# Group sums by identity products, reciprocals back in two transfers, and a planner that counts instruction blocks

## The chip, the core and the metric

The kernel runs on one core of a Trainium2 chip. The metric is the device time of one execution in microseconds, the median of the runs shown. Five engines take part: TensorE (PE; its weight loads are listed as PEld), VectorE (DVE), ScalarE (ACT), GpSimd (POOL) and SyncE (SP), which only issues transfers. Each runs its own list of instructions in order and waits on semaphores for the others.

## The reference

Two stages. The first is an attention with two parts per head (8 batches, 8 heads, 576 tokens, 64 columns); the second is an MLP over all 4608 tokens.

```
q_d, k_d, v_d = means over groups of 4 tokens             # 144 rows
out_d    = softmax(q_d k_d^T / 8) v_d, each row repeated 4 times
local    = softmax(q k^T / 8 where |i - j| < 4, else -1e9) v
x        = out_d + local            -> (4608, 512)
h        = x w_in                   # w_in (512, 2048)
out      = (h * sigmoid(h)) w_out   # w_out (2048, 512)
```

## The kernel before

The 64 heads are worked on in 32 pairs, two heads on the two halves of 128 rows. For a pair p the jobs have these names in the code:

- T: 36 transposes of q and k into PSUM (L807); e: the two copies of them to the tiles qT and kT (L837); for the first 12 pairs (GS_PE) also the sums over groups of 4 tokens, in the same PSUM banks, as 60 small matmuls against a permuted identity (idp, L809 to L824), copied to qd and kd (jobs mq, mk, L843). Later pairs form these sums on VectorE from qT and kT (L852).
- S: the scores (L866); x and xd: the exponentials on ACT (L897), tiles Pt and Pd.
- Z: the row sums of the exponentials by 14 matmuls (L955); r: their reciprocals on VectorE, tile zr (L969).
- PV: the products with v (L935, L948); m: the multiply of PV's result by the reciprocals, tile xo (L1020), which also frees PV's two PSUM banks; a: the sum of both parts on POOL into xT (L1047), the input of the MLP.

The multiply needs the reciprocals spread over rows and columns, tile Rb. The first 8 pairs (RB_PE) do that on TensorE: two corrections of zr on VectorE (L973), 20 matmuls (L994) and a copy (L1004). All later pairs do it by two transfers that ACT issues: zr to a scratch in DRAM (scr, L980), and, once that has landed, scr to Rb (L983). The source pattern of the second is 2 halves x 64 repeats x 720 numbers.

The MLP is cut into 9 blocks of 512 tokens. A G1 job is 4 matmuls of 128x512 (L1068), a tanh on ACT (th, L1073) and a product on VectorE (gT, L1077), which frees its PSUM bank; apart from the first and last block only two banks serve G1. A G2 job is 4 matmuls of 128x512 (L1098); 16 matmuls form one result, which ACT copies (osb, L1105) and SP stores.

Pairs 0 to 7 run as separate jobs. From pair 8 on, a visit V(n) on TensorE holds S of n, T of n+1, Z of n-1 and PV of n-2, and about 8 MLP jobs of 4 matmuls stand between two visits. PV and Z of a visit use one pair of banks (CD), so a visit can't begin its PV before the multiply of the previous visit's pair has run.

The order on every engine is written out when the kernel is built: a planner (class Plan, its loop at L324 to L476) takes jobs with costs, due times (D, L52) and pools of buffers, plays them through and appends each job's instructions to its engine's list. Nothing is reordered when it runs. Loads of q, k and v come from SP in the order of load_order (L99), with gates; three pairs of q and k and all weights come from POOL's queue. While TensorE is idle early on, the planner puts in matmuls on a constant tile (dz, L1273 to L1277).

All matmuls of TensorE but the transposes are recorded by one helper, so they have the line L557; copies have L551, transfers L671.

Of the kernel before, what the change touches and what calls it, by code (L numbers as in the profile page):

```python
# [20 lines left out]
WARM_END, WARM_GAP, WARM_PART = 115.0, 0.4, 0.6  # L21
# [12 lines left out]
K_ENG = "DVE"  # L34
FRESH = 2.2


def Z_ENG(p):
    return "ACT"
# [12 lines left out]
def D(p, left):  # L52
    return (22 + 2 * (p - 3) if p < 4 else 42 + 3 * (p - 7) if p < 8 else 45 + 8 * (p - 7)) - left
# [45 lines left out]
def load_order():  # L99
    o = ["kx", ("qk", 0), ("qk", 1), ("qk", 2), ("qk", 3), ("v", 0), ("v", 1), ("v", 2), ("v", 3)]  # L100
    for p in range(4, NPAIR):
        o += [("qk", p), ("v", p)] + ([("vq", p)] if p >= VP_PE else [])
    return o, {1: ["ck1"], **{p: ["lv311!"] for p in range(4, 8)}, 8: ["w2"]}
# [8 lines left out]
def LD_ENG(x, p):  # L112
    return "SP"
# [129 lines left out]
class Job:  # L243
    __slots__ = ("name", "eng", "cost", "emit", "pre", "take", "use", "due", "work", "port", "kind", "bank", "marks", "gran",
                 "idx", "n", "succ", "start", "end", "ran", "last", "thr", "idle")

    def __init__(self, name, eng, cost, emit, **kw):
# [7 lines left out]
        self.ran, self.last, self.succ, self.end, self.idle = None, None, [], None, None  # L255


class Plan:
# [65 lines left out]
    def run(self, pick):  # L324
# [25 lines left out]
        busy = {e: 0.0 for e in Prog.ENGS}  # L350
        ported = {"DVE": 0.0, "POOL": 0.0}
        queues = {e: [] for e in Prog.ENGS}
        fluid = [0.0, 0]
# [60 lines left out]
        def dispatch(e, now):  # L414
# [14 lines left out]
            if e == "PE":  # L429
                b = min((b for b in range(8) if self.banks[b] is None), key=lambda b: self.freed[b], default=None)  # L430
                if b is not None:
                    j.idle = (now - max(busy["PE"], self.freed[b]), b)
            self.grab(j)
            start = now
            if j.port and e in ported:
                start = max(now, ported["POOL" if e == "DVE" else "DVE"])
            j.ran, j.start = e, now
            cost = j.cost[e] * (COLD[1] if e == "PE" and now < COLD[0] else 1.0)
            end = start + cost
            busy[e] = end  # L440
# [21 lines left out]
        at(0.0, lambda: None)  # L462
# [16 lines left out]
def bass_hourglass_attn__then__act_silu_kernel(  # L479
# [9 lines left out]
    with kctx:  # L489
# [37 lines left out]
        zr = sb("zr", [128, 72], F32, N_ZR)  # L527
        Rb = sb("Rb", [128, 720], F32, N_RB)
# [16 lines left out]
        idp = sb("idp", [128, 64], BF16)  # L545
# [25 lines left out]
        kx, rkx = region(2048, 576)  # L571
        cpv = cp.rearrange("p (a b) -> p a b", a=2)
# [3 lines left out]
        def col(i):  # L576
            return cv[:, i:i + 1]
# [16 lines left out]
        def fill(name, parts, due, eng=("DVE", "POOL")):  # L594
            def emit(j):
                for dst, val, r, w in parts:
                    P.op(j.ran, lambda e, dst=dst, val=val: e.memset(dst, val), r, w)
            J(name, eng, {"DVE": 0.07 * len(parts), "POOL": 0.14 * len(parts)}, emit, due=due)

        def constants():  # L600
# [5 lines left out]
            ts("ch", col(CH), col(CP_), 64.0, ALU.is_ge, 1.0, ALU.mult, rc(CP_), rc(CH), 0.07, ["cp"], -100)  # L606
            ts("cb", col(CB), col(CH), -64.0, ALU.mult, 0.0, ALU.add, rc(CH), rc(CB), 0.07, ["ch"], -99)
            ts("cwb", col(CW), col(CH), 224.0, ALU.mult, -4.5, ALU.add, rc(CH), rc(CW), 0.07, ["ch"], -95)
            ts("ck", col(CK), col(CP_), col(CB), ALU.add, 0.0, ALU.add, rc(CP_, CB), rc(CK), 0.07, ["cb"], -95)
            ts("idn", idn[:, :], ci, col(CB), ALU.add, 0.0, ALU.is_equal, rc(CB) + ri, [R("idn")], 0.15,  # L610
               ["ci", "cb"], -98)
            ts("coa", col(CO), col(CK), 3.0, ALU.is_ge, 1.0, ALU.mult, rc(CK), rc(CO), 0.07, ["ck"], -50)
            ts("co2", col(CO2), col(CK), 58.5, ALU.is_le, col(CO), ALU.mult, rc(CK, CO), rc(CO2), 0.07, ["coa"], -50)
            ts("co", col(CO), col(CK), 60.5, ALU.is_le, col(CO), ALU.mult, rc(CK, CO), rc(CO), 0.07, ["co2"], -50)
            ts("ce0", col(CE0), col(CP_), 3.0, ALU.is_ge, 1.0, ALU.mult, rc(CP_), rc(CE0), 0.07, ["cp"], -60)
            ts("ce1", col(CE1), col(CP_), 123.0, ALU.is_lt, 1.0, ALU.mult, rc(CP_), rc(CE1), 0.07, ["cp"], -60)
            ts("ga", col(GA), col(CK), 10.0, ALU.is_ge, -1.0, ALU.mult, rc(CK), rc(GA), 0.07, ["ck"], -40)
            ts("gb", col(GB), col(CK), 20.0, ALU.is_ge, -1.0, ALU.mult, rc(CK), rc(GB), 0.07, ["ck"], -40)

            def size(name, x, b, rx, rb, cost, pre, due):  # L620
# [4 lines left out]
            const("gsel", "DVE", 0.12, lambda e: e.tensor_copy(idp[:, :].rearrange("p (b a) -> p b a", b=4),  # L625
                                                               idn[:, :].rearrange("p (a b) -> p b a", b=4)),
                  r=[R("idn")], w=[R("idp")], pre=["idn"], due=-90)
            for i, (a, b, c, rr) in enumerate(((0, 58, col(CE0), rc(CE0)), (58, 232, 1.0, []),
                                               (232, 288, col(CE1), rc(CE1)))):
                ts(f"mask{i}", mask[:, a:b], cm[:, a:b], 3.0, ALU.is_le, c, ALU.mult, rr + rm, [R(f"mask{i}")], 0.15,  # L630
                   ["cma"] + (["ce0", "ce1"] if rr else []), -20)
            ts("cm0", col(CM0), col(CK), 3.0, ALU.is_lt, 100.0, ALU.mult, rc(CK), rc(CM0), 0.07, ["ck"], -94)
            ts("cm1", col(CM1), col(CK), 59.0, ALU.is_ge, 100.0, ALU.mult, rc(CK), rc(CM1), 0.07, ["ck"], -94)
            ts("nidn", nidn[:, :], idn[:, :], -81920.0, ALU.mult, 0.0, ALU.add, [R("idn")], [R("nidn")], 0.1, ["idn"], -85)
            for i, (y, a, b, c) in enumerate(((0, 0, 58, CM0), (0, 58, 288, None), (1, 0, 232, None), (1, 232, 288, CM1))):
                if c is None:
                    ts(f"mb{i}", mbias[:, y, a:b], cm[:, a:b], 3.0, ALU.is_gt, 1.0, ALU.mult, rm, [R(f"mb{i}")], 0.25,
                       ["cma"], -84)
                else:
                    ts(f"mb{i}", mbias[:, y, a:b], cm[:, a:b], col(c), ALU.add, 3.0, ALU.is_gt, rc(c) + rm, [R(f"mb{i}")],  # L640
                       0.12, ["cma", "cm0", "cm1"], -84)
            for i, c in enumerate((CO, CO, CO2)):
                ts(f"vsel{i}", vsel[:, i, :], cpv[:, i % 2, :], 1.5, ALU.is_le, col(c), ALU.mult, rc(c) + rp,
                   [R(f"vsel{i}")], 0.22, ["cpa", "co", "co2"], -70)
            ts("rsela", rsel[:, :], idn[:, 0:10], 1.0, ALU.mult, 0.0, ALU.add, [R("idn")], [R("rsel")], 0.07, ["idn"], -60)
            for i in (1, 2):
                const(f"rsel{i}", "DVE", 0.07, lambda e, i=i: e.tensor_tensor(
                    rsel[:, :], rsel[:, :], idn[:, 10 * i:10 * i + 10], ALU.add), r=[R("idn"), R("rsel")],
                    w=[R("rsel")], pre=["rsela" if i == 1 else "rsel1"], due=-60)
# [5 lines left out]
                 + [(hot[64 * j:64 * j + 16, 2, 13 + 5 * j:34 + 5 * j:10], 4.0, [rW[2]], [rW[2]]) for j in range(2)], -72,  # L655
                 "DVE")
            fill("ohf", [(ohf[:, 0:30], 0.0, [], [R("ohf")]), (ohf[:, 30:64], 1.0, [], [R("ohf2")])]
                 + [(ohf[half(j), 5 * j:5 * j + 21:10], 1.0, [R("ohf")], [R("ohf")]) for j in range(2)], -71, "DVE")
# [139 lines left out]
        def pe_T(p):  # L798
            a, b = S("qkb", p), S("qkb", p - 1)
            grp = p < GS_PE  # L800
# [8 lines left out]
            if grp:  # L809
                for r in range(9):  # L810
                    cs = [(9 * b_ + r) // 4 for b_ in range(4)]
                    runs, b0 = [], 0
                    for b_ in range(1, 5):
                        if b_ == 4 or cs[b_] - cs[b_ - 1] != 2:
                            runs.append((b0, b_))
                            b0 = b_
                    for a_, e_ in runs:
                        for j, h, x, n in tiles:
                            t = t_home(p, x, 0)[0]
                            o = PS[half(h), t, 288:432].rearrange("p (c a) -> p c a", c=9)  # L820
                            c0 = cs[a_]
                            mm(o[:, c0:c0 + 2 * (e_ - a_) - 1:2, :], qkb[n][half(j), x, 64 * r:64 * r + 64],
                               idp[half(j), 16 * a_:16 * e_].rearrange("p (b a) -> p b a", a=16),
                               [R("idp"), R(f"qkb{n}{x}")], [rB[t]], r == 0, r == 8)  # L824

        def after_T(p):
# [12 lines left out]
            def group(x):  # L839
                def emit(jb):  # L840
                    s, b = S("T", p), bank(("qk"[x], p))[0]
                    dst = qd[s][:, :] if x == 0 else kd[s][:, 0:SD]
                    P.op(jb.ran, lambda e: copy(jb.ran, e, dst.rearrange("p (a c) -> p a c", c=9),  # L843
                                                PS[:, b, 288:432].rearrange("p (c a) -> p a c", c=9)),
                         [rB[b]], [R(f"{'qk'[x]}d{s}")])
# [9 lines left out]

            for x in range(2):
# [3 lines left out]
                if grp:  # L860
                    J(f"m{n}{p}", G_ENG(p, x), {"ACT": 0.31, "DVE": 0.27}, group(x), pre=[f"T{p}"], bank=[((n, p), ())],
                      due=D(p, 8.0), **keys)
# [103 lines left out]
        def after_Z(p, key, i, col_):  # L966
            def emit(jb):
                z, b = S("zr", p), bank(key)[i]
                P.op("DVE", lambda e: e.reciprocal(zr[z][:, :], PS[:, b, col_:col_ + 72]), [rB[b]], [R(f"zr{z}")])  # L969
                if p < RB_PE:  # L970
                    hi = zr[z][:, :].bitcast(BF16)[:, 1:144:2]
                    for g in (GA, GB):
# [3 lines left out]
            J(f"r{p}", "DVE", 1.27 if p < RB_PE else 0.6, emit, pre=[f"Z{p}"] + (["ga", "gb"] if p < RB_PE else []),  # L976
              bank=[(key, ())], take=[("zr", p)], due=D(p, 4.0))
            if p < RB_PE:
# [4 lines left out]
            dma(f"b{p}0", Z_ENG(p), lambda: Rb[S("Rb", p)][:, :],  # L983
                lambda: bass.AP(tensor=scr[S("Rb", p)].tensor, offset=scr[S("Rb", p)].offset,
                                ap=[[64 * 72, 2], [0, 64], [1, 720]]),
                lambda: [R(f"scr{S('Rb', p)}")], lambda: [R(f"Rb{S('Rb', p)}")],
                lambda: f"Rb{S('Rb', p)}", 1.0, 0.43, gran=0.114, pre=[f"z{p}"], use=[("Rb", p)], due=-1000 + p, kind="hot")

        def pe_RB(p):
            z, bb = S("zr", p), bank(("r", p))  # L990
            hi = zr[z][:, :].bitcast(BF16)[:, 1:144:2]
            for c in range(10):
                for h in range(2):
# [320 lines left out]
```

## Time and profile before

| | |
|---|---|
| median of 3 runs | 515.62 us (513.09 to 517.13) |
| profiled execution | 517.7 us, span from first to last instruction 515.9 us |
| busy PE, DVE, ACT, POOL | 386.2, 224.8, 170.2, 155.8 us |
| mean granted TensorE clock | 0.858 of full |
| first G1 of block 0 | 43.0 us |
| first visit's scores (S8) | 84.0 us |
| last multiply (pair 31) ends | 425.5 us |

How to read it: the span is of one execution. Busy shares are averages over stages with different limits, so the text goes stage by stage. The chain that ended last is followed back from the last instruction; "issue" in it is time in which an engine waited for nothing that the profile shows. The granted clock is the share of TensorE's full clock that the chip allowed.

### The profile page before, as it was taken

The numbers are of one execution on the slowest core, as the hardware profiler recorded it, in microseconds if no ns is written. First come the engines' busy times: TensorE is split into PE (matmuls) and PEld (weight loads), VectorE is DVE, ScalarE is ACT, GpSimd is POOL, SyncE is SP. The second block draws the span as 40 slices with busy tenths as digits, with TensorE's granted clock in tenths as the row PEclk, the third lists the DMA queues.
The fourth block names the chain that finished last, engine by engine and source line by source line (L and its number), as shares of the span: only waits on it lengthen the run. The fifth ranks groups of instructions, "written<-read, shape, count | busy, mean of one in ns | idle before, by whom it ended". The sixth has DMA issues, their size and how long they took to land.

```text
span 515.9 us, 12557 instructions
## 1 busy us (share of the span) xinstructions
PE 386.2 (75%) x5521; PEld 239.6 (46%) x5556; DVE 224.8 (44%) x387; ACT 170.2 (33%) x307; POOL 155.8 (30%) x182
## 2 busy tenths in 40 slices
PE   6668788719536587578658785888588659999997
PEld 2556566515314354245334453555345335666543
DVE  6454476516414255325534454466455223344310
ACT  4324546413111232133313333334234113344421
POOL 4236248405535254413234443443201000000000
PEclk9557989978877668787887899789999878999999
DMA  8885995932774556756644443311211110111012
GB/s 176 207 218 167 228 246 126 241 83 67 200 198 126 146 137 172 187 141 179 159 137 139 133 127 101 104 60 51 71 42 64 62 51 22 41 42 41 20 62 81
DMA packets 77104, 62.61 MB, mean 121 GB/s; under 512 B 49402, under 2 KB 59898, under 8 KB 77050
## 3 DMA queue, kind: packets, MB, share of 16 engines
q1 hardware_dynamic: 65386, 44.91, 32.5%
q0 software_dynamic: 5088, 7.18, 6.5%
q10 hardware_dynamic: 6576, 9.73, 5.7%
q8 instruction: 43, 0.70, 0.7%
q14 instruction: 11, 0.09, 0.1%
HBM read 54.46 MB, written 10.32 MB: 126 GB/s over the span
## 4 chain that ended last, share of the span: by engine, by line
DMA 52%; PE 35%; DVE 8%; issue 4%; ACT 1%; DVEq 0%; ACTq 0%
DMA Rb<-scr 41%; PE PS L557 34%; DMA scr<-zr 11%; DVE xo L1020 3%; DVE zr L969 1%; DVE gT L1077 1%; PE PS L807 1%; DVE zr L973 0%; ACT kT L551 0%; DVE qT L551 0%; DVE mbias L592 0%; ACT th L1073 0%; DVE vsel L592 0%; DVE cv L592 0%; DVE qd L852 0%
## 5 line engine op out<-in xcount | busy, mean ns | idle before, releaser
L557 PE MATMUL PS<-xT,w_in_sb 128*128 128x512 f32 x576 | 193.7, 471 | 65.9 <-DVE gT L1077 64.9
L557 PEld LDWEIGHTS PS<-xT,w_in_sb 128*128 128x128 f32 x576 | 119.5, 215 | 108.7 <-DVE gT L1077 75.6
L1073 ACT ACTIVATE th<-PS 128x512 f32<-128x512 f32 x144 | 85.8, 598 | 221.2 <-PE PS L557 158.2
L557 PE MATMUL PS<-w_out_bf,gT 128*128 128x512 bf16 x546 | 146.4, 409 | 3.7 <-issue 2.4
L1077 DVE SCALAR_TENSOR_TENSOR gT<-th,PS 128x512 bf16<-128x512 f32 x144 | 96.8, 681 | 78.0 <-ACT th L1073 73.8
L1047 POOL TENSOR_TENSOR xT<-xo 128x576 fp32r<-128x576 f32 (+3 forms) x48 | 42.0, 889 | 198.0 <-DVE xo L1020 198.0
L557 PEld LDWEIGHTS PS<-w_out_bf,gT 128*128 128x128 bf16 x576 | 52.5, 104 | 79.3 <-issue 33.5
L1020 DVE TENSOR_TENSOR xo<-PS,Rb 128x720 f32<-128x720 f32 x32 | 29.0, 907 | 137.9 <-DMA Rb<-scr 132.0
L551 POOL CAST vb<-vs 128x640 bf16<-128x640 f32 x32 | 23.4, 733 | 66.8 <-PE PS L557 56.9
L1105 ACT ACTIVATE osb<-PS 128x512 f32<-128x512 f32 x36 | 21.5, 597 | 57.5 <-PE PS L557 41.5
L551 DVE COPY qT<-PS 128x576 bf16<-128x576 bf16 x29 | 21.9, 756 | 35.1 <-PE PS L807 23.4
L557 PE MATMUL PS<-Pt,vb 64*64 64x58 bf16 (+1 forms) x640 | 12.8, 209 | 29.6 <-DVE xo L1020 29.6
L767 POOL CAST qkb<-qk 128x1152 bf16<-128x1152 f32 x28 | 32.5, 1165 | 1.4 <-DMA qk<-in_k_dram 1.4
L780 POOL TENSOR_TENSOR vt<-vq 128x512 f32<-128x512 f32 x24 | 31.7, 1322 | 0.4 <-POOL vd L785 0.3
L897 ACT ACTIVATE Pt<-PS 128x576 bf16<-128x576 f32 x32 | 20.7, 648 | 20.7 <-PE PS L557 12.1
L557 PEld LDWEIGHTS PS<-Pt,vb 64*64 64x64 bf16 x640 | 9.7, 123 | 32.4 <-DVE xo L1020 30.8
L969 DVE RECIPROCAL zr<-PS 128x72 f32<-128x72 f32 x32 | 19.2, 600 | 10.4 <-PE PS L557 10.3
L897 ACT ACTIVATE Pd<-PS 128x432 bf16<-128x432 f32 x32 | 17.1, 533 | 10.4 <-DMA scr<-zr 10.4
L551 ACT ACTIVATE kT<-PS 128x576 bf16<-128x576 bf16 x28 | 18.6, 664 | 0.0
L785 POOL TENSOR_TENSOR vd<-vt 128x256 bf16<-128x256 f32 x24 | 18.1, 752 | 0.5
L807 PE MATMUL PS<-idn,qkb 64*64 64x64 bf16 x1152 | 16.7, 203 | 1.2 <-DVE qkb L551 0.8
L557 PEld LDWEIGHTS PS<-qT,kT 64*64 64x64 bf16 x640 | 9.8, 117 | 15.6 <-issue 14.6
(69 smaller groups left out, 273.1 us busy)
## 6 DMA issues: line engine op xcount, KB each, us to landing
vs<-in_v_dram SPq DMA_DIRECT2D x126, 80.0 KB, 5.9
out_dram<-osb SPq DMA_DIRECT2D x36, 256.0 KB, 3.7
Rb<-scr ACTq DMA_DIRECT2D x24, 360.0 KB
qk<-in_q_dram SPq DMA_DIRECT2D x29, 288.0 KB, 5.5
qk<-in_k_dram SPq DMA_DIRECT2D x28, 288.0 KB, 6.5
vq<-in_v_dram SPq DMA_DIRECT2D x24, 256.0 KB, 6.6
w_in_sb<-in_moe_w_in_dram POOLq DMA_DIRECT2D x4, 1024.0 KB, 7.8
w_out_bf<-in_moe_w_out_dram POOLq DMA_DIRECT2D x4, 512.0 KB, 7.9
```

Source lines behind the costliest of these rows:

```text
L551: return e.activation(out_, in_, AF.Copy) if eng == "ACT" else e.tensor_copy(out_, in_)
L557: P.op("PE", lambda t: t.matmul(out_, lhsT, rhs, start=start, stop=stop, skip_group_check=True), r, w)
L767: P.op("POOL", lambda e, a=i(), b=j(): e.tensor_copy(qkb[b][:, :, :], qk[a][:, :, :]), [R(f"qk{i()}0"), R(f"qk{i()}1")], [R(f"qkb{j()}0"), ...
L780: P.op("POOL", lambda g: g.tensor_tensor(vt[:, :, :], vq[n][:, :, 0:128], vq[n][:, :, 128:256], ALU.add), [R(f"vqm{n}"), R(f"vqe{n}0"), R( ...
L807: P.op("PE", lambda e, o=o, w=w, j=j: e.transpose(o, w, idn[half(j), :]), [R("idn"), R(f"qkb{n}{x}")], [rB[t]])
L897: P.op("ACT", lambda e: e.activation(d[:, :, :], PS[:, b[0]:b[1] + 1, a:e_], AF.Exp, scale=sc), [rB[b[0]], rB[b[1]]], [R(f"P{m}" if local ...
L969: P.op("DVE", lambda e: e.reciprocal(zr[z][:, :], PS[:, b, col_:col_ + 72]), [rB[b]], [R(f"zr{z}")])
L1020: P.op("DVE", lambda e: e.tensor_tensor(xo[x][:, :, :], PS[:, bb[0]:bb[1] + 1, 0:360], Rb[u][:, :].rearrange("p (x c) -> p x c", x=2), ALU ...
L1047: P.op("POOL", lambda g, dst=dst, in0=in0, in1=in1: g.tensor_tensor(dst, in0, in1, ALU.add), [R(f"xo{x}")], xblk(kc, t + a, t + e_))
L1073: P.op("ACT", lambda e: e.activation(th[x][:, :], PS[:, b, :], AF.Tanh, scale=0.5), [rB[b]], [R(f"th{x}")])
L1077: P.op("DVE", lambda e: e.scalar_tensor_tensor(gT[j % 2][:, f, :], th[x][:, :], 1.0, PS[:, b, :], ALU.add, ALU.mult), [rB[b], R(f"th{x}")] ...
L1105: P.op("ACT", lambda e, s=S("osb", n), b=bank(key)[0]: e.activation(osb[s][:, :], PS[:, b, :], AF.Copy, scale=0.5), [rB[bank(key)[0]]], [R ...
```

## The change

Five things.

1. Group sums (first 12 pairs). The 60 small matmuls inside T go. A new job G comes after the two copies e: 8 matmuls against a 128x128 block identity (idw), 4 for q and 4 for k, which add up every fourth column of qT and kT in a PSUM bank of its own. The copies to qd and kd follow G.
2. Spread of the reciprocals on TensorE (first 8 pairs). 10 matmuls over all 128 rows against a stored weight tile rw, which lies in a part of gT that is free early on, instead of 20 over 64 rows. The corrections of zr are a job of their own, on VectorE or POOL.
3. Spread by transfers (pairs 8 to 31). Rb is read by two transfers, one for each half of 64 rows. The multiply waits for both.
4. Planner. It counts TensorE's instructions in blocks of 256 with a delay per block, starts the engines at small offsets, has new costs for constants and for filling matmuls, and other due times.
5. Loads and constants. v of pair 1 may be issued by SP or ACT and has no gate; some constants are due later.

```diff
-WARM_END, WARM_GAP, WARM_PART = 115.0, 0.4, 0.6
+WARM_END, WARM_GAP, WARM_PART, WARM_COLD = 115.0, 0.4, 0.6, 7.0
+FETCH = (4.5, 110.0, 3.7)
+R_ENG = ("DVE", "POOL")
...
-    return o, {1: ["ck1"], **{p: ["lv311!"] for p in range(4, 8)}, 8: ["w2"]}
+    return o, {**{p: ["lv311!"] for p in range(4, 8)}, 8: ["w2"]}
...
-    return "SP"
+    return ("SP", "ACT") if p in (1,) else "SP"
+
+
+def G_BANKS(p):
+    return ((4,), (5,), (6,), (7,), (3,), (2,))
...
+            if e == "PE" and j.mm:
+                left_, t, per = 2 * j.mm, start, cost / (2 * j.mm)
+                while left_:
+                    n = min(left_, code[2] - code[0])
+                    t, left_, code[0] = t + per * n, left_ - n, code[0] + n
+                    if code[0] == code[2]:
+                        t = max(t, code[1])
+                        code[1], code[2] = t + (FETCH[0] if t < FETCH[1] else FETCH[2]), code[2] + 256
...
+            fill("rwz", [(rwf, 0.0, [], rrw)], 6.0, "POOL")
+            for j in range(2):
+                const(f"rw{j}", "ACT", 0.72, lambda e, j=j: e.activation(
+                    rw[half(j), :, 64 * j:64 * j + 64], rsel[half(j), :].unsqueeze(2).to_broadcast([64, 10, 64]), AF.Copy),
+                    r=[R("rsel")] + rrw, w=[R(f"rw{j}")], pre=["rsel2", "rwz"], due=8.8)
...
-            if grp:
-                for r in range(9):
...
-                            mm(o[:, c0:c0 + 2 * (e_ - a_) - 1:2, :], qkb[n][half(j), x, 64 * r:64 * r + 64],
-                               idp[half(j), 16 * a_:16 * e_].rearrange("p (b a) -> p b a", a=16),
-                               [R("idp"), R(f"qkb{n}{x}")], [rB[t]], r == 0, r == 8)
+
+        def pe_G(p):
+            s, b = S("T", p), bank(("g", p))[0]
+            for x, t in enumerate((qT[s][:, :], kT[s][:, 3:579])):
+                for r in range(4):
+                    mm(PS[:, b, 144 * x:144 * x + 144], idw[:, :], t.rearrange("p (g r) -> p r g", r=4)[:, r, :],
+                       [R("idw"), R(f"{'qk'[x]}T{s}")], [rB[b]], r == 0, r == 3)
...
+            if grp:
+                J(f"G{p}", "PE", 0.62, lambda jb: pe_G(p), pre=[f"eq{p}", f"ek{p}", "idw1"], bank=[(("g", p), G_BANKS(p))],
+                  due=D(p, 7.7), use=[("T", p)], kind="A", mm=8)
...
-            dma(f"b{p}0", Z_ENG(p), lambda: Rb[S("Rb", p)][:, :],
-                lambda: bass.AP(tensor=scr[S("Rb", p)].tensor, offset=scr[S("Rb", p)].offset,
-                                ap=[[64 * 72, 2], [0, 64], [1, 720]]),
...
+            for h in range(2):
+                dma(f"b{p}{h}", Z_ENG(p), lambda h=h: Rb[S("Rb", p)][half(h), :],
+                    lambda h=h: bass.AP(tensor=scr[S("Rb", p)].tensor, offset=scr[S("Rb", p)].offset + 64 * h * 72,
+                                        ap=[[0, 64], [1, 720]]),
...
             for c in range(10):
-                for h in range(2):
-                    mm(PS[half(h), bb[c // 5], 72 * (c % 5):72 * (c % 5) + 72],
-                       rsel[half(h), c:c + 1].to_broadcast([64, 64]), hi[half(h), :], [R("rsel"), R(f"zr{z}")],
-                       [rB[bb[c // 5]]], True, True)
+                mm(PS[:, bb[c // 5], 72 * (c % 5):72 * (c % 5) + 72], rw[:, c, :], hi[:, :],
+                   rrw + [R("rw0"), R("rw1"), R(f"zr{z}")], [rB[bb[c // 5]]], True, True)
...
-            J(f"m{p}", "DVE", 0.92, emitm, pre=[f"PV{p}", f"b{p}0"], bank=[(("o", p), ())], use=[("Rb", p)],
+            J(f"m{p}", "DVE", 0.92, emitm, pre=[f"PV{p}", f"b{p}0", f"b{p}1"], bank=[(("o", p), ())], use=[("Rb", p)],
```

## The prediction

> **What bounds the kernel now.** I read the page's chain first, then the DMA queues, then the waits of the stretch in which attention and the MLP run together, then busy time by stage.
>
> ```profile
> DMA 52%; PE 35%; DVE 8%; issue 4%; ACT 1%; DVEq 0%; ACTq 0%
> q10 hardware_dynamic: 6576, 9.73, 5.7%
> Rb<-scr ACTq DMA_DIRECT2D x24, 360.0 KB
> ```
>
> The chain that ends last runs through transfers for half of the span, though queue 10, which carries them, has 5.7% of the engines' time. By line, Rb<-scr is 41% and scr<-zr 11%: the way of the reciprocals from the SBUF tile zr to DRAM (scr) and back, spread, to Rb. The 6576 packets show why it is slow: they are 24 x (128 + 16 + 128 + 2). In the packet list a scr write is 128 packets of 288 B and 16 of 4 B, an Rb read 128 of 2880 B and only 2 of 4 B, never more than two of the 2880 B ones at a time. I read the 4 B packets as one closing mark per engine: the Rb read uses 2 of 16 engines. Its packets take 0.114 us each, 64 x 0.114 = 7.3 us at least; first to last packet is 7.8 to 12.7 us.
>
> ```profile
> DVE xo L1020 <- DMA Rb<-scr: 132.0, 24, 12.3
> PE PS L557 <- DVE gT L1077: 59.8, 17, 6.2
> PE PS L557 <- DVE xo L1020: 29.6, 5, 10.8
> ```
>
> These are waits from 114 to 425 us. VectorE stands at the multiply xo (L1020) 5.5 us per pair; behind it in its queue stands gT (L1077), which empties the two PSUM banks of the first MLP product; so TensorE waits 59.8 us for gT and 29.6 us for xo itself. The next scr write also has its shares behind the Rb packets on those two engines: pair 9's write began at 101.58 and ended at 114.16, just after Rb of pair 8 (114.03). So Rb reads follow each other at 13.6 us per pair ((415.2 - 101.3)/23).
>
> ```profile
> 84.00:128.00 44.00, 28.00 (x619) 19.37 (x626) 20.84 (x33) 15.54 (x30) 18.41 (x23) 0.88 0.62 145
> 128.00:396.60 268.60, 189.57 (x2592) 114.20 (x2614) 120.74 (x183) 80.70 (x145) 98.00 (x107) 0.84 0.46 128
> 396.60:515.90 119.30, 104.44 (x566) 60.03 (x568) 34.71 (x52) 37.95 (x64) 3.65 (x3) 0.94 0.13 47
> 436.70:512.70 76.00, 75.60 (x336) 42.87 (x340) 22.51 (x33) 26.96 (x46) 0.00 (x0) 1.00 0.12 45
> ```
>
> Columns: stretch, length, busy PE, PEld, DVE, ACT, POOL, granted clock, DMA share, GB/s. Stage 1 (0 to 84.0) is pairs 0 to 7; stage 2 visits V8 to V11; stage 3 the 19 visits V12 to V30; stage 4 the rest, from V31. In stage 3 no engine is full: PE is idle 79 us and its clock is 0.84, against 75.6 of 76 us at 1.00 in the pure MLP at the end.
>
> Stage 1 has another limit.
>
> ```profile
> 10.97 2.31 issue
> 13.28 0.35 PE PS L557 x14
> 13.63 0.29 PE PS L807 x35
> 13.92 1.20 PE PS L557 x75
> 15.11 2.44 issue
> 17.56 2.06 PE PS L557 x35
> ```
>
> TensorE stops without any wait and goes on at 13.28, 17.56 and 22.17, and between the first two are 128 matmuls, with their weight loads 256 instructions: one 16 KB packet of queue 8 (43 packets, 0.70 MB). The stalls end 4.28 and 4.61 us apart: 4.4 us per 128 small matmuls, however short they are.
>
> **The change, part by part.**
>
> Rb in two transfers of 64 rows. In each the leading dimension of the source is the 64 repeats, no longer the 2 halves. Nearest row: the first load of the kernel, 64 rows of 2304 B, has 16 closing packets and lands 2.6 us after its issue; 256 KB output stores over 128 rows take 3.7. With 0.51 us more for the second issue on ACT: 3.1 to 4.2 us, I take 3.5, against 12.2 (median on the chain). Bounds: nothing gained if 16 engines reading one row of DRAM share what one engine got; 3.1 at best. ACT pays one more issue, 24 x 0.51 = 12 us; behind it stands th (L1073), and ACT is busy 80.7 of 268.6 us.
>
> The Trainium skill has two rules here, which disagree. "DMA: Bandwidth & Descriptors", section "Rules for kernel authors", says of two transfers to disjoint partition halves that they are not worth it, since each sprays over all 16 engines anyway; by this the split saves nothing. The same section says that a leading zero-stride or short dimension confines a transfer to as many engines as that dimension counts. The two closing packets side with the second; only after this will the first hold.
>
> What is late next in stages 2 to 4? From zr to xo the way becomes reciprocal 0.6, write 1.5 (its least) to 4.0, read 3.5, wake-up 0.5: 6 to 8.6 us, then xo 0.9. The bank that the next but one visit wants is thus free well within two visits. What is left is TensorE's own order. The built orders give the MLP matmuls between visits: 84 from S8 to S12, 564 from S12 to S31, 436 after it (before: 72, 576, 436). One takes 76.0/336 = 0.226 us at full clock (last window above); a whole visit 1.31 us (339.73 to 341.04).
> - Stage 3: 564 x 0.226 + 19 x 1.31 = 152.5 us. VectorE needs 120.7/19 = 6.4 us per pair, POOL 5.2, ACT 4.2 + 0.5, all under 8.0. I add 0.95 us per pair for ACT standing before the Rb issue until scr lands (th behind it, then gT, then TensorE): 171 us, 9.0 per pair. The visit at 340 came within 9.0 of the next one once its 1.33 us stall is taken out. From 268.6: -98. Loads: queue 1 has 32.5% of the span, 168 us of all engines, 5 us per pair, so they keep up.
> - Stage 2: 84 x 0.226 + 4 x 1.31 + 2 for the new group products = 26, + 3 for the first Rb: 29, against 44.
> - Stage 4: 436 x 0.226 + 2.3 for the last three visits + 3.2 from the last matmul to the end = 104, against 119.3.
>
> The clock is in these sums: after the 10.8 us wait at 104.6 the clock fell to 0.50 (110 to 120 us), while at 440 to 500 us it is 1.00. The skill's "TensorE: Matmul & The Clock Gate", section "Part 1: The HAM clock gate", gives about 3.4 us of idleness as what halves it; waits of 1 us would be harmless by that.
>
> Group sums (L809 to L824 to pe_G). Per pair 60 small matmuls go and 8 of 128x144 come, 12 pairs; the spread of reciprocals (L994) goes from 20 to 10 matmuls, 8 pairs. Before the first S8 matmul the built order has 1249 matmuls instead of 1794. At 4.4 us per 128, 545/128 x 4.4 = 18.7 us. Bounds: zero if loads or VectorE's chain set the pace, 25 by the stage's mean pace (5.8 us per 128). Against it: the sums now wait for the copies of the transposes (0.76), the products and another copy (0.31), 1.3 us of latency more per pair, beside other pairs' work; and DMA share reached 1.10 and 1.15 in 20 to 30 and 60 to 70 us. I take 14: stage 1 ends at 70. Strided columns in the new products: nearest is zr,rsel with 231 ns against 222 for Pd,vd; 96 matmuls, nothing.
>
> The skill speaks against this: "Runtime: NRT & Kernel Launch", section "Instruction fetch mechanics", calls the crossing of a 16 KB block mostly hidden. By it fewer instructions give nothing, and stage 1 would end near 84. The stalls above decide for me.
>
> Small parts, together between -2 and +2 us, taken as 0: constants move behind the first casts on VectorE (the first cast ran at 7.45 after constants), 3 more warming matmuls of 0.43 us stand before the first transposes, two ACT copies and one POOL clear build the spread weights, POOL takes some of the zr corrections (its queue holds the weight issues behind), v of pair 1 is issued by ACT (4 issues off SP), planner costs move jobs.
>
> **Sum.** 70 + 29 + 171 + 104 = 374 us of span; the run had 1.8 outside it: 376, against 517.7. The median of the runs (515.62) is 0.996 of that: 374.
>
> **Rivals.**
> - *Reads spread, queues still stall* (0.22). VectorE and ACT take work in a fixed order; a late xo or scr landing stops gT. For: gT is TensorE's largest wait now. Against: at 340 a visit needed 9.0. At 11 us per pair: 19 x 2.0 = 38 more, 412.
> - *Better than that* (0.09): the 0.95 per pair is hidden (-18) and stage 1 gains 25 (-11): 345.
> - *The split does not spread or one DRAM row serves no faster* (0.05). Then xo waits as now and only stage 1 gains: 515.6 - 14 = 502.
> - *Slower* (0.03): 16 engines reading the same row hold each other up, and the loads on the same engines with them. Eight packets per engine and pair; stages other than these reads need 234 us of the engines (45%) less 29. It decides from (516 - 205)/24 = 13 us per pair, 1.6 us per packet instead of 0.114; at 1.9 us it is 570. Against it: one engine read one row again and again at full packet rate.
> - *Forecast* (0.60): 355 to 396.
> - No change (0.01).
>
> About 1% is what a measurement can tell. Faster 0.96, same 0.01, slower 0.03. The range 345 to 428 holds forecast, better and the stalled-queue case.
>
> **What would show it.** Right: queue 10 at 24 x (128 + 16 + 2 x 80) = 7296 packets, Rb from issue to xo near 4 us, xo <- Rb waits under 30 us, granted clock over 0.95 from 128 us on, 9 us per pair, S8 near 70. Wrong: Rb packets still two at a time; PE waiting for gT over 40 us in the middle; S8 still after 78, with loads as what ended the waits.

## The result, and the profile after

The changed kernel takes **384.94 us** (median of 4 runs, 384.14 to 386.0), the kernel before beside it 514.36: a ratio of 0.749, 95% interval 0.7432 to 0.7547. The forecast was 374 with a range of 345 to 428. The profiled execution took 384.23 us, its span is 382.4. Here and below, times are medians of the fast runs, and ratios are of fast runs too: a run that took over 1.5% longer than the fastest of the same kernel is left out. By the stages of the prediction (after's are cut at 68.2, 103.0 and 279.5 us, each within 0.2 us of the first matmul of S8, S12 and S31):

| | before | forecast | after |
|---|---|---|---|
| stage 1, to the first matmul of S8 | 84.0 | 70 | 68.2 |
| stage 2, S8 to S12 | 44.0 | 29 | 34.8 |
| stage 3, S12 to S31 (per pair) | 268.6 (14.1) | 171 (9.0) | 176.5 (9.29) |
| stage 4, from S31 | 119.3 | 104 | 102.9 |
| mean granted clock | 0.858 | over 0.95 from 128 us on | 0.978 |

The page after, its parts on the chain (shares of the span), the DMA queues and the DMA issues:

```profile
PE 68%; DMA 21%; DVE 6%; issue 3%; ACT 1%; ACTq 0%; SPq 0%; DVEq 0%
...
q10 hardware_dynamic: 8304, 9.98, 9.6%
...
Rb<-scr ACTq DMA_DIRECT2D x48, 180.0 KB, 4.6
```

TensorE is now 68% of the chain; the DMA share went from 52% to 21%. Queue 10 has 7296 packets of the reciprocals and 1008 of v of pair 1, which ACT issues now: 960 of 256 B and 3 x 16 closing ones. The 7296 are 24 x (128 + 16 + 128 + 32): two Rb reads with 16 closing packets each where there were 2. From the first to the last 2880 B packet an Rb takes 3.23 us in the median, before 9.15; in the median read 16 packets are under way at the peak, before 3.

The waits from 66 to 300 us (us in total, times, longest):

```profile
DVE xo L1055 <- DMA Rb<-scr: 15.8, 10, 4.4
PE PS L583 <- DVE gT L1112: 15.7, 9, 3.5
...
DVE xo L1055 <- issue: 7.5, 5, 3.1
```

The three waits that carried the kernel before were 132.0, 59.8 and 29.6 us; two are 15.8 and 15.7, and TensorE's wait for xo itself is 0.9. The five waits at xo that are put down to "issue" end 0.6 to 0.9 us after the last packet of their Rb, so they read as waits for Rb as well. VectorE thus still stands at xo, for 23.3 us and at 15 of the 24 pairs instead of all, and gT behind it still stops TensorE.

Busy time in stages 2, 3 and 4 (length, PE, PEld, DVE, ACT, POOL, granted clock, DMA share, GB/s):

```profile
68.20:103.00 34.80, 30.07 (x489) 19.69 (x485) 19.24 (x30) 16.30 (x33) 20.47 (x26) 0.95 0.90 213
103.00:279.50 176.50, 161.17 (x2603) 100.31 (x2594) 121.16 (x184) 79.97 (x145) 94.73 (x103) 0.99 0.71 189
279.50:382.40 102.90, 99.71 (x576) 57.51 (x566) 34.94 (x52) 38.02 (x64) 3.66 (x3) 1.00 0.15 54
```

In stage 3 PE's idle time fell from 79 to 15.3 us and the clock rose from 0.84 to 0.99. Of the 92.1 us by which the stage got shorter, 63.7 are idle time; the other 28.4 are busy time (189.57 to 161.17 us), with as many matmuls (2592 and 2603 recorded) at the better clock. The DMA share rose from 0.46 to 0.71: much the same loads in two thirds of the time. Of the 32.1 us that PE is still idle in the whole span, 20.1 lie in stages 2 and 3. Finer windows show where:

```profile
103.00:140.00 37.00, 32.39 (x638) 20.41 (x626) 26.25 (x38) 16.83 (x31) 27.15 (x31) 1.00 0.97 254
140.00:180.00 40.00, 30.47 (x429) 17.80 (x426) 22.34 (x34) 14.27 (x26) 20.22 (x21) 1.00 1.02 251
180.00:220.00 40.00, 38.85 (x561) 24.65 (x562) 28.01 (x44) 18.48 (x33) 21.83 (x25) 0.96 0.72 194
220.00:280.00 60.00, 59.96 (x1017) 37.91 (x1017) 44.91 (x70) 30.89 (x56) 25.53 (x28) 1.00 0.33 104
```

PE stands idle for 14.1 of the 77 us from 103 to 180, while the DMA share is about 1; from 220 us on the loads are done and PE is idle for 0.04 us. The chain just before these stretches and in the first of them (start, us, what) is still the way of the reciprocals:

```profile
76.09 6.68 DMA scr<-zr
82.80 0.49 ACTq L706
83.33 7.77 DMA Rb<-scr
91.19 0.92 DVE xo L1055
...
113.21 5.14 DMA scr<-zr
118.37 0.45 ACTq L706
118.85 5.01 DMA Rb<-scr
123.96 0.91 DVE xo L1055
```

Once the loads are done, the Rb packets of the last six pairs take 2.20 us from first to last. So the experiments have three questions: which part of the change made the gain of stages 2 to 4, what shortened stage 1, and what holds the 20 us of idle time that are left.

### The profile page after: what moved, and what is told of

Its sections match the earlier page's. It is cut to its first block, busy times and chain, and to the rows that moved or that the text cites. A ratio compares the mean times of both kernels' runs of the same rounds, so it can differ in the third digit from the quotient of the medians.

```text
span 382.4 us, 11248 instructions
## 1 busy us (share of the span) xinstructions
PE 350.3 (92%) x4853; PEld 220.1 (58%) x4853; DVE 224.6 (59%) x383; ACT 170.5 (45%) x308; POOL 161.3 (42%) x196
## 4 chain that ended last, share of the span: by engine, by line
PE 68%; DMA 21%; DVE 6%; issue 3%; ACT 1%; ACTq 0%; SPq 0%; DVEq 0%
PE PS L583 66%; DMA Rb<-scr 11%; DMA scr<-zr 8%; PE PS L841 2%; DVE xo L1055 2%; DMA qk<-in_k_dram 2%; DVE zr L1003 1%; DVE gT L1112 1%; DVE zr L996 1%; DVE Pt L930 1%; ACTq L706 0%; ACT th L1108 0%; DVE qT L577 0%; ACT osb L1140 0%; SPq L706 0%
## 5 line engine op out<-in xcount | busy, mean ns | idle before, releaser
L583 PE MATMUL PS<-xT,w_in_sb 128*128 128x512 f32 x576 | 171.1, 428 | 16.0 <-DVE gT L1112 15.7
L583 PE MATMUL PS<-w_out_bf,gT 128*128 128x512 bf16 x576 | 138.4, 381 | 0.4 <-DVE qT L577 0.3
L583 PEld LDWEIGHTS PS<-xT,w_in_sb 128*128 128x128 f32 x576 | 106.7, 191 | 50.0 <-DVE gT L1112 23.3
L583 PEld LDWEIGHTS PS<-w_out_bf,gT 128*128 128x128 bf16 x576 | 49.8, 98 | 69.1 <-issue 16.9
L1055 DVE TENSOR_TENSOR xo<-PS,Rb 128x720 f32<-128x720 f32 x32 | 28.9, 902 | 24.3 <-DMA Rb<-scr 15.8
L802 POOL CAST qkb<-qk 128x1152 bf16<-128x1152 f32 x28 | 33.3, 1188 | 4.0 <-DMA qk<-in_k_dram 3.9
L815 POOL TENSOR_TENSOR vt<-vq 128x512 f32<-128x512 f32 x24 | 32.1, 1335 | 6.2 <-DMA vq<-in_v_dram 5.9
L577 ACT ACTIVATE kT<-PS 128x576 bf16<-128x576 bf16 x30 | 20.1, 669 | 0.4 <-PE PS L841 0.2
L930 DVE TENSOR_TENSOR Pt<-Pt,mask 128x576 bf16<-128x576 bf16 x24 | 17.0, 710 | 0.9 <-ACT Pt L924 0.9
L841 PEld LDWEIGHTS PS<-idn,qkb 64*64 64x64 bf16 x1152 | 13.2, 111 | 4.1 <-DVE qkb L577 2.2
L583 PE MATMUL PS<-Pd,vd 64*64 64x72 bf16 (+1 forms) x256 | 14.5, 202 | 0.8 <-issue 0.8
```

Source lines behind the costliest of these rows:

```text
L577: return e.activation(out_, in_, AF.Copy) if eng == "ACT" else e.tensor_copy(out_, in_)
L583: P.op("PE", lambda t: t.matmul(out_, lhsT, rhs, start=start, stop=stop, skip_group_check=True), r, w)
L802: P.op("POOL", lambda e, a=i(), b=j(): e.tensor_copy(qkb[b][:, :, :], qk[a][:, :, :]), [R(f"qk{i()}0"), R(f"qk{i()}1")], [R(f"qkb{j()}0"), ...
L815: P.op("POOL", lambda g: g.tensor_tensor(vt[:, :, :], vq[n][:, :, 0:128], vq[n][:, :, 128:256], ALU.add), [R(f"vqm{n}"), R(f"vqe{n}0"), R( ...
L841: P.op("PE", lambda e, o=o, w=w, j=j: e.transpose(o, w, idn[half(j), :]), [R("idn"), R(f"qkb{n}{x}")], [rB[t]])
L1055: P.op("DVE", lambda e: e.tensor_tensor(xo[x][:, :, :], PS[:, bb[0]:bb[1] + 1, 0:360], Rb[u][:, :].rearrange("p (x c) -> p x c", x=2), ALU ...
```

## The experiments

### One part alone, and the change without it

The kernel before, with nothing but the two transfers (one job issues both, so TensorE's order is the same as before):

```diff
-            dma(f"b{p}0", Z_ENG(p), lambda: Rb[S("Rb", p)][:, :], ... ap=[[64 * 72, 2], [0, 64], [1, 720]]),
+            def emitb(j):
+                for h in range(2):
+                    P.op(j.ran, lambda s, h=h: s.dma_start(Rb[S("Rb", p)][half(h), :], bass.AP(
+                        tensor=scr[S("Rb", p)].tensor, offset=scr[S("Rb", p)].offset + 64 * h * 72, ap=[[0, 64], [1, 720]])),
...
```

> The kernel before, with one edit: the read of Rb is two transfers of 64 rows each, issued one after the other by ACT in the same job; planner, order on every engine and all matmuls as before. Theory A (the read on two engines paced pairs 8 to 31; spreading it is nearly all of the gain): S8 stays near 84 us, from there as in the changed kernel (34.8 + 176.5 + 102.9 us), so a span of about 400, range 393 to 412. Theory B (the gain comes from the new order, fewer instructions and the better clock that follows): above 490.

Measured: 401.13 us, ratio 0.7822 (0.7747 to 0.7896). Stage 1 is 83.5, as before; stages 2 to 4 are those of the changed kernel. Stages 3 and 4 of it:

```profile
119.40:297.20 177.80, 166.37 (x2616) 102.55 (x2612) 121.96 (x183) 80.06 (x145) 97.39 (x106) 0.96 0.73 193
297.20:400.00 102.80, 99.66 (x572) 57.46 (x560) 34.94 (x52) 37.93 (x64) 3.66 (x3) 1.00 0.15 52
```

177.8 and 102.8 against 176.5 and 102.9: nothing else of the change is needed for them.

The other way round, the changed kernel with its own order, and the Rb read issued as one transfer again:

```diff
-                                        ap=[[0, 64], [1, 720]]),
+                        ap=[[64 * 72, 2], [0, 64], [1, 720]])),
```

> The changed kernel, with one edit: Rb is read by one transfer of 2 halves x 64 repeats again, in the place of the first of the two; plan and order are the same. Theory A: S8 stays near 68, then 13 to 14 us per pair as before: about 499, range 488 to 512; queue 10 shows 2 closing packets per read. Theory B: under 410.

Measured: 505.22 us, ratio 0.9859 (0.9782 to 0.9935). The old waits are back (100 to 400 us):

```profile
DVE xo L1058 <- DMA Rb<-scr: 114.5, 21, 9.5
...
PE PS L583 <- DVE gT L1115: 71.1, 16, 7.4
```

Stage 1 keeps its gain (66.9), but of the 17 us 9 are lost again in stage 3 (277.3 against 268.5). Without the split the rest of the change is worth 9 us (514.4 to 505.2), with it 16 (401.1 to 384.9). Why stage 3 is longer here than before was not followed up.

### The number of engines

The two transfers stay, the 64 repeats are written as 2 x 32 or as 4 x 16: same bytes, same 128 packets, another leading dimension.

```diff
-                                        ap=[[0, 64], [1, 720]]),
+                                        ap=[[0, 2], [0, 32], [1, 720]]),      # e3;  [0, 4], [0, 16] in e4
```

> The changed kernel, with one edit: still two transfers of 64 rows, but the 64 repeats in the source are written as 2 x 32, so that the leading dimension is 2. If the number of engines is what counts (2 closing packets each, both halves on the same two engines), as with one transfer: about 499, range 488 to 515. If it is that there are two transfers, or that the multiply waits for halves: like the changed kernel, 385.

> As the 2 x 32 form, but 4 x 16: leading dimension 4. Theory A: 128 packets on four engines, 32 x 0.116 = 3.7 us at least and perhaps 6 with other traffic, against 2 to 4.6 us first to last in the changed kernel: the read is then no longer the longest part of the way, so 385 to 400. If every engine fewer costs in proportion, about 430.

| leading dimension | closing packets of an Rb | packets at once, peak of the median read | first to last packet, median | last six pairs | stage 3 per pair | time |
|---|---|---|---|---|---|---|
| 2 halves, one transfer (e2) | 2 | 3 | 9.35 us | 8.60 | 14.59 | 505.2 |
| 2, two transfers (e3) | 2 x 2 | 3.5 | 9.72 us | 8.60 | 15.08 | 523.3 |
| 4, two transfers (e4) | 2 x 4 | 6 | 5.63 us | 4.88 | 11.48 | 435.8 |
| 64, two transfers (after) | 2 x 16 | 16 | 3.23 us | 2.20 | 9.29 | 384.9 |

Two transfers by themselves gain nothing: with 2 x 32 they cost 9.72 us and the whole is 523.25, slightly slower than before (ratio 1.0199, 1.007 to 1.0328; two runs, a little above what was expected). What counts is the leading dimension of the source, as the Trainium skill's "DMA: Bandwidth & Descriptors" has it in "Rules for kernel authors". The closing packets, 2, 4 and 16 per transfer, read as its number of engines: the peaks and the times of the table go with them. Both transfers of e3 have about as many packets under way at once as the one of e2, so by this reading they share their two engines. The last six pairs, without loads beside them, fit 0.114 us x packets per engine + 1.2: 64 x 0.114 + 1.2 = 8.5, 32 x 0.114 + 1.2 = 4.8, 8 x 0.114 + 1.2 = 2.1, where the 1.2 was chosen to fit the three.

The 435.83 us of e4 decide another point. If the way of the reciprocals had fallen off the path as soon as it was shorter than a visit, e4 would have come out near 385 to 400. It came out in proportion, and its waits (100 to 330 us) say that VectorE still stands at xo; those put down to "issue" end 0.4 to 1.2 us after the last packet of their Rb:

```profile
DVE xo L1055 <- issue: 41.4, 13, 6.8
PE PS L583 <- DVE gT L1112: 34.5, 15, 6.3
```

Nearly each microsecond of the read is paid for, from 9.7 down to 3.2: (15.08 - 9.29) / (9.72 - 3.23) = 0.89 us of a pair per us of the read.

### Stage 1: the number of matmuls

The changed kernel, with the 60 old products of T put back for its 12 pairs, into free columns of the same banks; nobody reads them. 540 more matmuls stand before S8 (1789 instead of 1249). The order is that of after; the copies of T's result wait for the new matmuls too, which share its banks.

```diff
+            for r in range(9):
+                ...
+                for a_, e_ in (runs if p < GS_PE else ()):
+                    for j, h, x, n in tiles:
+                        mm(o[:, c0:c0 + 2 * (e_ - a_) - 1:2, :], qkb[n][half(j), x, 64 * r:64 * r + 64], idp[...], ..., r == 0, r == 8)
```

> The changed kernel, and in each T of the first 12 pairs the 60 small matmuls of the old group sums again, into the PSUM columns that they had; nothing reads them (one more small copy on VectorE for their weights; order otherwise the same). Before S8 540 more matmuls. Theory F (stage 1 goes at about 4.4 us per 128 small matmuls, whatever they compute): S8 from 68 to 82 to 87, time near 403. Theory L (the sum over stage 1 is set by waits between engines, and extra matmuls cost only what TensorE takes for them, 0.67 us per T): S8 at 72 to 75, time near 391.

Measured: 399.1 us, ratio 0.7787 (0.7667 to 0.7908). S8 starts at 83.4, 15.2 us later: 3.6 us per 128 matmuls, their own time included. Stages 2 to 4 stay (35.5, 177.6, 102.9). TensorE's waits that are put down to "issue", first in the kernel before (0 to 95 us), then in after (0 to 85), then two lines of this one (0 to 85):

```profile
PE PS L557 <- issue: 16.7, 10, 3.3
...
PE PS L583 <- issue: 4.0, 4, 2.8
...
PE PS L584 <- issue: 10.2, 10, 2.5
PE PS L847 <- issue: 4.1, 2, 3.2
```

"issue" is TensorE standing with nothing to wait for: 14.3 us here, 10.3 more than in after. Its other waits are 1.8 us shorter, so its idle time before S8 grows by 8.5 us (8.9 to 17.4); the other 6.7 are busy time (59.35 to 66.03), the extra matmuls' own. One such stand is left in the early stretch of after's chain (start, us, what):

```profile
20.24 3.52 PE PS L583 x127
23.77 2.77 issue
26.53 0.82 PE PS L583 x23
```

The other way: the new G job taken out, the old sums in T used again.

```diff
-                J(f"G{p}", "PE", 0.62, lambda jb: pe_G(p), pre=[f"eq{p}", f"ek{p}", "idw1"], ..., mm=8)
-            J(f"T{p}", "PE", 0.4, lambda jb: pe_T(p), mm=36, ...)
+            J(f"T{p}", "PE", 0.85 if p < GS_PE else 0.4, lambda jb: pe_T(p), mm=36 + 60 * (p < GS_PE), ...)
```

> The changed kernel with the old group sums in T (60 matmuls, copies to qd and kd straight from T's banks) and no job G; the planner is told of it, so the order is its own. Before S8 462 more matmuls. Theory F: S8 at 80 to 86, time 395 to 405. Theory L, with the copies' 1.3 us less on the way of each pair: S8 at 66 to 70, time 380 to 388.

Measured: 406.02 us, ratio 0.792 (0.7848 to 0.7991), just above the range. S8 is at 81.1 with 1711 matmuls before it: 12.9 us for 462 more, again 3.6 per 128. The part that was not expected is stage 4, 109.9: in this order 684 MLP matmuls stand before S31 instead of 716, and 32 x 0.226 = 7.2 us have moved from one stage to the other.

The Trainium skill's "Runtime: NRT & Kernel Launch", section "Instruction fetch mechanics", calls the cost of an instruction block mostly hidden; here 540 matmuls brought 10.3 us more of standing still. The traces show what TensorE stands for. Count its instructions (matmuls, weight loads and its few waits) from the start, and look at each stand of over 0.3 us before S8. In the kernel before, 9 of 9 end after 449 instructions or a multiple of 256 more (449, 705, 961 and so on, to within the 3 that missing records make), in after 2 of 2, in the kernel with the unread products (e6) 9 of 10, and 8 of 9 in the one with the old sums (e7). Each of these 28 ends 1.2 to 1.8 us after a 16 KB packet of queue 8 has ended, and queue 8 has one such packet per 256 of TensorE's instructions: 38 in after, which make 9728, for 9706 matmuls and weight loads. So what TensorE stands for is its next block of 256 instructions.

### The planner

A part of the fourth thing in the change never happens: the planner, although it is written to, counts no job's instructions and adds no delay per block. A job is given its number of matmuls and loses it in the next statement: the constructor sets the keywords and then `self.ran, ..., self.mm, self.fill = None, ..., 0, None` (L261). The condition `if e == "PE" and j.mm` is never met. With the zero set before the keywords, it counts:

```diff
+        self.mm = 0
-        self.ran, self.last, self.succ, self.end, self.mm, self.fill = None, None, [], None, 0, None
+        self.ran, self.last, self.succ, self.end, self.fill = None, None, [], None, None
```

> In the changed kernel a job's number of matmuls (mm) is set from its keywords and then set to 0 in the same constructor, so the planner never counts a block. Here the 0 comes first: the counting works, and the order on all engines is another. If stage 1 is bound by blocks, knowing them should help the order: S8 3 to 6 us earlier, 378 to 383. If TensorE is held by the blocks in any order: within 1% of 385.

Measured: 387.9 us, ratio 0.7569 (0.7458 to 0.768): no gain shown, 3 us above after, with intervals that overlap. Stage 1 is 70.3 us, stage 3 is 2.6 us shorter and stage 4, at 109.9, 7.0 longer: here too 32 matmuls have moved behind S31. S8 is not earlier, and the time lies within 1% of 385, as the second case had it; but its reason, that the blocks hold TensorE in any order, does not fit. Up to 85 us TensorE stands only 0.7 us with nothing to wait for, 4.0 in after, and other waits have come in the place of these (0 to 85 us):

```profile
PE PS L584 <- POOL zr L1010: 5.1, 2, 4.3
...
PE PS L584 <- issue: 0.7, 2, 0.5
```

Then the costs: the planner takes 0.2 us for the write to scr and 0.5 for each half of Rb. It is told 1.0 and 1.5.

```diff
-... lambda: f"scr{S('Rb', p)}", 0.2, 0.43, gran=0.019,
+... lambda: f"scr{S('Rb', p)}", 1.0, 0.43, gran=0.019,
-... lambda h=h: f"Rb{S('Rb', p)}{h}", 0.5, 0.45, gran=0.114,
+... lambda h=h: f"Rb{S('Rb', p)}{h}", 1.5, 0.45, gran=0.114,
```

> The changed kernel, planner alone: it is told 1.0 us of transfer for scr (0.2 before) and 1.5 us for each half of Rb (0.5 before), nearer to what the trace shows (first to last packet 3.2 us for both halves), so that it puts the Rb issue and the multiply later in ACT's and VectorE's order. Theory A' (what is left above TensorE's own work in stages 2 and 3 is VectorE and ACT standing at transfers that the order places too early): 9.3 us per pair falls to 8.5 to 8.9, time 370 to 378. Rival (TensorE is full, 92% busy): 385, no change; or slower, since the multiply comes late for the next visit: above 390.

Measured: 383.82 us, ratio 0.7507 (0.7414 to 0.7599). Stages 3 and 4:

```profile
100.90:265.30 164.40, 149.50 (x2538) 94.69 (x2559) 115.96 (x174) 76.00 (x134) 95.40 (x105) 0.98 0.79 204
265.30:382.10 116.80, 112.88 (x625) 65.17 (x622) 39.34 (x58) 43.37 (x73) 4.88 (x4) 1.00 0.15 53
```

The time is that of the rival, no change. The pace of 8.65 us per pair is what was hoped for, and it is worth nothing: 60 MLP matmuls that stood between visits now stand behind S31, and 60 x 0.226 = 13.6 us went to stage 4. The pace per pair is a wrong measure when the order changes; TensorE's idle time is the right one, 14.9 us in this stage 3 and 15.3 in that of after.

### What holds the rest: the loads

Two ways to thin the loads out. First, without the loads of vq (v as the group means read it) for pairs 10 to 31, which leaves that part of the output out:

```diff
+                    if p >= VP_PE + N_VQ:
+                        return
```

> The changed kernel without the vq loads of pairs 10 to 31 (the sums of v over 4 tokens are then made from what lies in the two buffers, so that part of the output is left out); all compute instructions and their order as before. 22 x 320 KB fewer, about a quarter of the loads. Theory C (what stays above TensorE's own work between 68 and 180 us is that the scr and Rb transfers share 16 engines with the loads, which fill them there: DMA share 0.91 to 1.02, scr to Rb issue 5 to 6 us instead of 2.2 later): DMA share near 0.8, that stretch 8 to 14 us shorter, time 372 to 378. Rival (VectorE's and ACT's fixed order, transfers of any speed): within 3 us of the changed kernel.

Second, with all loads, but each pair's loads held back until the visit of an earlier pair has ended, so that they don't run ahead. The planner knows of this gate, so the order on the engines changes with it:

```diff
-    return o, {**{p: ["lv311!"] for p in range(4, 8)}, 8: ["w2"]}
+    return o, {**{p: ["lv311!"] for p in range(4, 8)}, 8: ["w2"], **{p: [f"V{p - 3}"] for p in range(12, NPAIR)}}
```

> As the gate at V(p-5), but at V(p-3), for pairs 12 to 31: some 18 us from release to the transposes, of which loads, cast and queueing take 10 to 12. Theory C: 374 to 381. If that is too late: above 390.

> The changed kernel, and the loads of pair p (14 to 31) wait for the end of visit V(p-5), so that they are spread over the visits instead of running ahead as far as buffers allow. Theory C: DMA share between 103 and 180 us falls to 0.75 to 0.9, time 375 to 382. Rival: 384 to 388. If a load then comes too late for its visit: above 390, with loads as what TensorE's feeders wait for.

And the changed kernel unaltered beside them, on the same chip:

> The changed kernel once more, unaltered, so that the next three are compared with it on the same chip: 384 to 388.

| | time | ratio to before | stage 3 | Rb, first to last packet |
|---|---|---|---|---|
| after again | 384.5 | 0.7442 (0.7385 to 0.7499) | 177.9 | 3.11 |
| without vq | 373.0 | 0.7268 (0.7188 to 0.7349) | 167.1 | 2.64 |
| loads after V(p-3) | 377.4 | 0.7311 (0.7264 to 0.7357) | 171.7 | 2.59 |
| loads after V(p-5) | 376.4 | 0.7314 (0.7248 to 0.738) | 173.6 | 2.61 |

After again, in the stretch with the most loads:

```profile
103.00:140.00 37.00, 27.63 (x409) 16.70 (x407) 20.72 (x34) 12.35 (x23) 25.70 (x30) 0.91 1.05 265
140.00:180.00 40.00, 36.22 (x550) 22.77 (x551) 26.48 (x40) 16.88 (x31) 22.07 (x22) 0.96 0.88 226
```

Without vq:

```profile
103.00:140.00 37.00, 31.46 (x525) 20.07 (x523) 23.68 (x37) 14.62 (x27) 25.60 (x30) 0.91 0.91 218
140.00:180.00 40.00, 39.71 (x573) 24.47 (x572) 30.53 (x48) 19.20 (x35) 25.66 (x25) 1.00 0.80 224
```

With the gates at p-3:

```profile
103.00:140.00 37.00, 33.36 (x609) 21.65 (x594) 26.47 (x39) 16.85 (x31) 23.06 (x26) 0.91 0.79 209
140.00:180.00 40.00, 37.85 (x563) 23.00 (x562) 28.77 (x44) 17.84 (x34) 20.33 (x20) 1.00 0.80 213
```

PE's idle time in these 77 us falls from 13.2 to 5.8 us without vq, and stage 3 gets 10.8 us shorter. TensorE, VectorE and GpSimd run the same instructions in the same order in this trace as in after's, so it is the loads: they held up the short transfers that the chain goes through. (GpSimd's own waits for vq, 5.9 us in after, are not on its chain.)

With the gates at p-3 the DMA share falls from 1.05 and 0.88 to 0.79 and 0.80, and PE's idle time in these 77 us to 5.8 us too. The same bytes are moved, later: the share in 220 to 280 us rises from 0.34 to 0.60. But from 115 us on TensorE's order is another than in after, so how much of the 6.2 us in stage 3 is the loads' and how much the order's was not separated. The gates at p-5 did not do what was expected of them: their share in the same stretches is 1.04 and 0.85, hardly lower, and PE idles 8.7 us. TensorE's order is that of after up to 150 us there, and yet S8 starts at 64.0 us instead of 66.6; that part of their gain, 2.7 us, is the spread of executions and not the gate's.

The two gated kernels, not told apart from each other, are the fastest complete ones of this study, 7 and 8 us or about 2% below the changed kernel beside them; both medians lie below its fastest run (380.84). What holds the last idle time of these kernels is open.

## Why the prediction was right or wrong

The direction, the mechanism and the range were right; 374 was 11 us too low. By its steps:

- **The Rb read, "I take 3.5".** The mechanism is shown: 32 closing packets, and e1 alone gives 113 of the 129 us. The size was off: issue to last packet is 4.70 us in the median and issue to the start of xo 5.91, against "near 4 us". Only from 226 us on, without loads beside it, does a read take 3.1 to 4.3 us from issue to last packet.
- **Stage 3, 171 against 176.5.** Worked out were 152.5 us of matmuls plus "0.95 us per pair", 18 us; the second term measured 24.0, of which 15.3 are idle time of TensorE and 8.7 matmul time above the 152.5. The step that failed is "Loads: ... 5 us per pair, so they keep up". They keep up, but the same loads in a shorter stage take the DMA share to 1, and on the chain from 113 to 180 us the scr write and the Rb read then take 3.7 to 7.4 us each. The cause that was named, ACT standing until scr lands, is on the chain (113.21 to 118.85), but what makes it long is the loads: without those of vq and with the same order, stage 3 lost 10.8 us beside its own comparison, 8.5 of them idle time.
- **Stage 2, 29 against 34.8.** The term "+ 3 for the first Rb" was mis-sized: pair 8's write took 6.68 and its read 7.77 us, with a DMA share of 0.90. PE's idle time in the stage is 4.7 us; the other 4 us are matmul time above the 26 that were counted. The clock of 0.95 explains 26 / 0.95 - 26 = 1.4 of it; the trace has 3.7 us of the new group products against the 2 that were counted, and 1.0 us of filling matmuls that were not. These overlap other matmuls, so the parts are upper bounds.
- **Stage 4, 104 against 102.9,** and "granted clock over 0.95 from 128 us on": right, 0.99 in stage 3 and 1.00 in stage 4. Of nine waits of TensorE of 0.9 us or more between 80 and 182 us in after, the two longest, 3.48 and 3.02 us, were followed by 3.4 us at half the clock, and the seven of up to 2.5 us were not. In the kernel before, the clock fell to half at waits of 1.6, 2.2 and 2.5 us too (at 72, 335 and 280 us), so a bound near 3.4 us does not come out of these traces. That waits of about 1 us are harmless does: at none of 0.9 to 1.4 us that began at full clock, in either trace, did it fall.
- **Stage 1, "I take 14", S8 "near 70": 68.2.** 545 fewer matmuls brought 15.8 us. The price "4.4 us per 128" was too high: the runs show 3.6 to 3.7, the matmuls' own time included. From 40 to 68 us PE is busy all the time in after, so there is less stall left to save than the early stretch suggested. The mechanism, blocks of instructions, is what the traces show.
- **"7296 packets"** missed the 1008 of v of pair 1; the change to ACT had been counted as issues, not as packets of queue 10.
- **"Small parts ... 0".** "Planner costs move jobs" passed over that the block counting has no effect. e8 and e9, two other orders, come out at 388 and 384 us: neither is told apart from after's 385.
- **Rivals.** *Reads spread, queues still stall* holds in part: VectorE still stands 23.3 us at xo and TensorE 15.7 for gT, at 9.29 us per pair rather than 11. *The split does not spread* is what e2 and e3 look like (505 and 523). *Slower*, by 16 engines on one row, fell: the median packet takes 0.116 us against 0.114, the mean 0.162 against 0.131. *Better than that* failed on both of its conditions: the 0.95 us per pair was not hidden, and stage 1 gained 15.8 us, not 25.
- **Small readings.** "Never more than two" packets at a time: in the trace of before it is two or one for 97% of the time, three or four for the rest. The median read on its chain is 11.9 us, not 12.2, and stage 1's mean pace 84.0 / 1794 x 128 = 6.0 us, not 5.8. None of them moves the forecast.

The two rules that the prediction weighed: that two transfers to halves are not worth it fails here (514 to 401 us), and holds in e3, where the leading dimension stays short; that instruction blocks are mostly hidden fails in stage 1, where TensorE stood without a wait for 14.3 us in e6 and 14.6 in e7, nearly all of it at their ends.

## What to carry to other kernels

Look at the closing packets of a transfer before its bytes: a queue with 5.7% of the engines' time set the pace of this kernel, because its reads had a leading dimension of 2. When a short transfer lies on the chain, count what shares the engines with it: a shorter stage packs the same loads closer, and loads that run ahead then take back part of the gain; the plans that held them back were 7 and 8 us faster here, with another order. When an engine stands with nothing to wait for, count its instructions up to that point: here the stands came every 256. And judge a new order by the idle time of the engine that is the bound, not by the pace of one stage.

## What the runs showed of the hardware that was not expected

- Two transfers with two engines each had 3.5 packets under way at the peak of the median read, one such transfer 3: they didn't take two pairs of engines (e3, e2).
- Without loads beside it, the time of a read from first to last packet went as 0.114 us per packet and engine plus 1.2 us, for 2, 4 and 16 engines, with all engines of a half on the same row of DRAM.
- A small write to DRAM (128 packets of 288 B) took 1.5 to 3.4 us from its issue to the issue that waits for it, 2.3 in the median, in the ten pairs from 215 us on, and 2.8 to 6.75, 5.7 in the median, in the ten pairs before 170 us, where the DMA share was 0.90 to 1.02 (after).
- 540 matmuls that nobody reads, put between others in the first 85 us, cost 15.2 us: TensorE stood 10.3 us more with nothing to wait for, at the ends of its blocks of 256 instructions but for under 1 us of it.
